# Frequency-domain 7x7 convolution: the last tile's turn, on chip or by DRAM

## The chip, the core and the metric

The kernel runs on one core of a Trainium2 chip. The core has a matrix engine (TensorE, PE in the profile; its weight loads are PEld), three engines for elementwise work (VectorE = DVE, ScalarE = ACT, GpSimd = POOL), a queue engine that mostly issues transfers (SyncE, SP) and 16 DMA engines. The metric is device time in microseconds of one execution; lower is better.

## The reference

```python
# x: (1, 224, 224, 96) bf16, w: (7, 7, 96, 96) bf16
wp = jnp.pad(w, ((0, H - K), (0, W - K), (0, 0), (0, 0)))
Xf = rfft2(x.astype(float32), axes=(1, 2))
Wf = rfft2(wp, axes=(0, 1))
Yf = jnp.einsum('bhwi,hwio->bhwo', Xf, Wf)
y = irfft2(Yf, s=(H, W), axes=(1, 2)).astype(bfloat16)
```

It is a circular 7x7 convolution of a 224x224 image, from 96 channels to 96 channels.

## The kernel before

The 224 rows are cut into `NJ` = 8 blocks of `B` = 28 rows. Each block, with its 6 rows of halo, is taken along the rows into `NS` = 17 frequencies (real and imaginary part: 34 numbers); along the columns the 7 taps are applied directly. The 224 columns are cut into 7 tiles (`NT`; the last is `TL` = 6) of 32 pixels, which are handled as 16 pairs `w`.

A tile goes through these stages:

- Forward transform (`a_jobs`, `f_jobs`): matmuls of the pixels in `xn` with `Fm`; the results are copied to `xf` by ScalarE or VectorE.
- `jit`: VectorE makes sums and differences of these planes in `J`.
- `b_round(t, s)`, one for each of the 17 frequencies s: TensorE multiplies `J` and `xf` with the transformed weights `WF` into two PSUM banks; ScalarE makes `tt_` of the first bank, VectorE makes `u` and `v`, and `ysum` adds them, on GpSimd or, where `ydve` is set, on VectorE. The result has 128 partitions (16 pairs x 8 blocks).
- Turn: the inverse transform contracts over the frequencies, so these have to get from the free dimension to the partitions. In tiles 0 to 5 the result is collected in `yf` (three frequencies a buffer, four buffers), stored to a DRAM tensor `scr`, and loaded from there into `tt` by `load_t`.
- Inverse transform (`c_jobs`): matmuls of `tt` with `G`, copies to `yo`, outputs to DRAM. Eleven such jobs belong to a tile; they run between the rounds of the next tile. `CQ[t]` says how many of the older and of the newer jobs run within the rounds of tile t; `queue_c` starts the loads of a tile.

Each engine takes its instructions in the order in which the program issues them (`_Ordered`). Nearly all transfers are issued by SP, one after the other: a transfer whose wait is not yet over holds those behind it.

The last tile has no next tile to hide its inverse transform. Before the change its turn is made on chip. `b_round` writes the sums of frequencies 0 to 12 (`SA` = 13) into `YA`, which lies in the free `xn`, and those of 13 to 16 into `YB`, in the free `xf` buffer, in an order in which 32x32 blocks can be transposed. `turn_a` (four VectorE transposes of 128x768, the first after the planes of round 13, the last within round 16) makes `TA` of `YA`; `turn_b` (two of 128x384, after the last round) makes `TB` of `YB`. In the tail `first` multiplies `TA` with `GA` (one matmul of 384 columns) and `second` adds four matmuls of 96 columns on `TB` with the four `GB`; there are 16 of each pair (8 blocks, 2 halves), and a copy to `tt` buffers by VectorE and ScalarE in turn follows each `second`. Eight `first` are issued ahead. Outputs are issued by SP, GpSimd and, the last, ScalarE. `GA` and `GB` lie in `GY`, 112 columns each (4 x 28 rows), built by `g_parts` during tiles 3 and 4. `warm` issues two matmuls that only keep TensorE busy.

In the profile every instruction carries the line of the recording helper (L86 before, L89 after), so operations are told apart by their tiles and shapes.

Of the kernel before, what the change touches and what calls it, by code (L numbers as in the profile page):

```python
# [8 lines left out]
BF16 = mybir.dt.bfloat16  # L9
F32 = mybir.dt.float32  # L10
# [4 lines left out]
B = 28  # L15
L = B + KT - 1
LC = L - 2
NS = L // 2
# [15 lines left out]
YGRP = ((0, 3), (3, 6), (6, 9), (9, 12), (12, 15), (15, 17))  # L34
SA = 13
NB4 = 4
YMAX = 3
YBUF = 4
JGB = ((0, 3), (3, 6), (6, 9), (9, 12), (12, 15), (15, 17))
LAG = 4  # L40
CQ = {2: (11, 0), 3: (11, 2), 4: (9, 5), 5: (6, 8), 6: (3, 8)}
SH2 = (0, 8, 13, 17)
MERGE = ()
NP2 = 0
# [9 lines left out]
def kernel(  # L54
# [85 lines left out]
    G = cpool.tile([3 * FR, 3 * B], BF16, name="Gm")  # L140
    SR = 32
    SRB = 2 * (NS - SA)
    assert 2 * SA <= SR and NB4 * SRB == SR and 4 * NJ == SR and B <= SR
    XW = 2 * TW * C
    xn_all = cpool.tile([128, 2 * (XW + 32)], BF16, name="xn")
    xn_bufs = [xn_all[0:R, i * (XW + 32):(i + 1) * (XW + 32)] for i in range(2)]
# [363 lines left out]
    def b_round(t, s, mid, end, ydve=False, planes=()):  # L510
# [5 lines left out]
            1: (Jb[:, 6], Jb[:, 3], Jb[:, 2]),  # L516
            2: (Jb[:, 5], Jb[:, 1], Jb[:, 0]),
        }
        if t == TL:
            yt, i = (YA, 2 * s) if s < SA else (YB, 2 * (s - SA))  # L520
            ym = yt[:, :, i:i + 2, :].rearrange("p g r o -> p g (r o)")
        else:
            for (y0, y1) in YGRP:
                if s == y0:
                    yf_cur[t] = (yf_pool.tile([128, YMAX, 2, 2, C], BF16, name="yf"), y0, y1)
            yf, y0, y1 = yf_cur[t]
            ym = yf[:, s - y0].rearrange("p r m o -> p m r o")
# [13 lines left out]
        if s in REAL:  # L541
            for part in range(2):
                conv(b0, part * C, 0, part)
            if t == TL:
                SE.copy(out=tt_.rearrange("p (r m o) -> p r m o", r=2, m=2),
                        in_=b0[:, 0:2 * C].rearrange("p (r o) -> p r o", o=C).unsqueeze(2).to_broadcast([128, 2, 2, C]))
            else:
                SE.copy(out=tt_[:, 0:2 * C], in_=b0[:, 0:2 * C])
            mid()
            for mi, m in enumerate((2, 1)):  # L550
                for part in range(2):
                    conv(b1, (part * 2 + mi if t == TL else mi * 2 + part) * C, m, part)
            if t == TL:
                VE.tensor_tensor(out=yp(ym), in0=pairs(tt_[:]), in1=pairs(b1[:, 0:4 * C]), op=ALU.add)
            else:
                VE.tensor_tensor(out=ym,
                                 in0=tt_[:, 0:2 * C].rearrange("p (r o) -> p r o", o=C).unsqueeze(1).to_broadcast([128, 2, 2, C]),
                                 in1=b1[:, 0:4 * C].rearrange("p (m r o) -> p m r o", m=2, r=2), op=ALU.add)
# [5 lines left out]
        else:  # L564
            v = tv_pool.tile([128, 2, 2, C], F32, name="v")
            if merge:
                conv(b0, 2 * C, 0, 0, both=True)
                conv(b0, 2 * C, 2, 0, add=True)
                conv(b0, 3 * C, 1, 0, add=True)
                conv(b0, 0, 0, 1)  # L570
                conv(b0, C, 0, 2)
                SE.mul(out=tt_[:], in_=b0[:, 0:4 * C], mul=-0.5)
                u, pr = tt_[:, 2 * C:4 * C].rearrange("p (m o) -> p m o", m=2), tt_[:, 0:2 * C]
            else:
                for part in range(3):
                    conv(b0, part * C, 0, part)
                conv(b0, 3 * C, 2, 0)
                conv(b0, 4 * C, 1, 0)
                u = tv_pool.tile([128, 2, C], F32, name="u")
                if t == TL:  # L580
                    SE.mul(out=tt_[:, 0:C], in_=b0[:, 0:C], mul=-0.5)
                    SE.copy(out=tt_[:, C:3 * C], in_=b0[:, C:3 * C])
                    load["a"] += 240
                else:
                    SE.mul(out=tt_[:, 0:3 * C], in_=b0[:, 0:3 * C], mul=-0.5)
                pr = tt_[:, C:3 * C]
# [3 lines left out]
            mid()  # L590
            for mi, m in enumerate((2, 1)):
                for pi, part in enumerate((1, 2)):
                    conv(b1, (pi * 2 + mi if t == TL else mi * 2 + pi) * C, m, part)
            if t == TL:
                VE.tensor_tensor(out=v[:], in0=pr.rearrange("p (r o) -> p r o", r=2).unsqueeze(2).to_broadcast([128, 2, 2, C]),
                                 in1=b1[:, 0:4 * C].rearrange("p (r m o) -> p r m o", r=2, m=2), op=ALU.add)
            else:
                VE.scalar_tensor_tensor(out=v.rearrange("p m r o -> p m (r o)"),
                                        in0=pr.unsqueeze(1).to_broadcast([128, 2, 2 * C]), scalar=-2.0,
                                        in1=b1[:, 0:4 * C].rearrange("p (m q) -> p m q", m=2), op0=ALU.mult, op1=ALU.add)  # L600
            def ysum(eng):
                if t == TL:
# [13 lines left out]
            load["a"] += 490 if merge else 410  # L616
            load["v"] += (560 if ydve else 250 if t < 2 else 0) + (560 if merge else 900)
            end()
        if t != TL and s == y1 - 1:
            dma(scr_tiles[t].rearrange("w j s e -> (w j) s e")[:, y0:y1], yf[:, 0:y1 - y0].rearrange("p s r m o -> p s (r m o)"))  # L620

    scr_tiles = {}
    tt_tiles = {}
# [14 lines left out]
    NA, NBL = C * SR * 2, C * SRB * 2  # L638
    xs = xf_bufs[(TL + 1) % 2].rearrange("c p r s w j -> c (p r s w j)")
    assert NA + 2 * NBL <= 4 * NS * POS * NJ and NA <= 2 * (XW + 32)  # L640
    YA = xn_all[:, 0:NA].rearrange("p (g s o) -> p g s o", s=SR, o=2)
    TA = xs[:, 0:NA].rearrange("p (g w j e) -> p w j g e", j=NJ, w=4, e=4)
    TB = xs[:, NA:NA + NBL].rearrange("p (g w j e) -> p w j g e", j=NJ, w=4, e=4)
    YB = xs[:, NA + NBL:NA + 2 * NBL].rearrange("p (g s o) -> p g s o", s=SRB, o=2)

    def turn(src, dst, g0, g1):
        load["v"] += 120 + 2 * SR * (g1 - g0) / 0.96
        VE.transpose(out=dst.bitcast(F32).rearrange("p (g n k) -> p g k n", n=SR, k=2)[:, g0:g1], in_=src[:, g0:g1])

    def turn_a(i):  # L650
        src = xn_all[:, 0:NA].bitcast(F32).rearrange("p (g k s) -> p g k s", k=2, s=SR)
        turn(src, xs[:, 0:NA], i * C // 8, (i + 1) * C // 8)

    def turn_b():
        load["v"] += 240 + C // NB4 * SR / 0.96
        src = xs[:, NA + NBL:NA + 2 * NBL].bitcast(F32).rearrange("p (g b k s) -> p k g b s", b=NB4, k=2, s=SRB)
        dst = xs[:, NA:NA + NBL].bitcast(F32).rearrange("p (g b j k) -> p k g b j", b=4, j=NJ, k=2)
        for k in range(2):
            VE.transpose(out=dst[:, k], in_=src[:, k])

    def g_parts():
        for q in range(4):
            dma(GX[q * SR:q * SR + 2 * SA, 0, q * B:q * B + B], G[0:2 * SA, 0:B])
            yield
        for q in range(4):
            for b in range(NB4):
# [1 line left out]
                dma(GX[r:r + SRB, 1 + b, q * B:q * B + B], G[2 * SA:2 * NS, 0:B])  # L668
                yield
        for k in range(NB4 + 1):  # L670
            GE.tensor_copy(out=GY[:, k].rearrange("p (m q) -> p q m", q=4), in_=GX[:, k].rearrange("p (q m) -> p q m", q=4))
            yield

    yo_free = [J_bufs[2][0:4 * B, i * PXC * C:(i + 1) * PXC * C] for i in range(2)]
# [120 lines left out]
    for r in range(NS + LAG):  # L795
# [18 lines left out]
        if r == PGRP[-2][1] + 1:  # L814
# [4 lines left out]
            yo_pool = ctx.enter_context(tc.tile_pool(name="yo", bufs=2, side="right"))  # L819
            g_pool = ctx.enter_context(tc.tile_pool(name="gp", bufs=1, side="right"))  # L820
            GX = g_pool.tile([128, 1 + NB4, 4 * B], BF16, name="GX")
            GY = g_pool.tile([128, 1 + NB4, 4 * B], BF16, name="GY")
            GA, GB = GY[:, 0], GY[:, 1:]
            GE.memset(GX[:], 0.0)
        if r == NS + 3:
            queue_c(0)
        for t in range(2):
# [14 lines left out]
    gp = g_parts()  # L842
    for t in range(2, NT):
        if t == TL:
            GE.memset(YA[:, :, 2 * SA:, :].rearrange("p g s o -> p g (s o)"), 0.0)
        else:
            scr_tiles[t] = dr_pool.tile([TW, NJ, NS, 4 * C], BF16, name="scr")
        qs = []
# [14 lines left out]
        for s in range(NS):  # L863
            now = ()
            if s in plan:
                g = plan[s]
                now = jit(t, g + 1) if g + 1 < len(JGB) else jit(t + 1, 0)
            if s == 3:
                queue_c(t - 1)
            if t in (3, 4):  # L870
                next(gp, None)
            mid = fills(qs, 2 * s)
            if t == TL and s >= SA:
                if s < NS - 1:
                    now = [lambda i=s - SA: turn_a(i)]
                else:
                    mid = lambda m=mid: (m(), turn_a(3))
            b_round(t, s, mid, fills(qs, 2 * s + 1), bool(now) and not (t == TL and s >= SA), now)
    turn_b()
    load["v"] = 2 * BIAS + load["a"]  # L880
    for f in cj:
# [8 lines left out]
    MO = 4 * B  # L890

    def first(j, h):
        pc = bank()[0:MO, 0:NC]
        TE.matmul(pc.rearrange("p (w g e) -> p w g e", w=2, e=4), lhsT=GA, rhs=TA[:, 2 * h:2 * h + 2, j], start=True, stop=False)
        return pc

    def second(j, h, pc, yo):
        po = pc.rearrange("p (w g b e) -> p b w g e", w=2, b=NB4, e=4)
        for b in range(NB4):
            TE.matmul(po[:, b], lhsT=GB[:, b], rhs=TB[:, 2 * h:2 * h + 2, j], start=False, stop=b == NB4 - 1)  # L900
        tail_evac(yo[0:MO, (j % 2) * 2 * NC + h * NC:(j % 2) * 2 * NC + (h + 1) * NC], pc, NC)
    order = [(j, h) for j in range(NJ) for h in range(2)]
    warm(WARM0)
    live = {k: first(*k) for k in order[:8]}
# [44 lines left out]
```

## Time and profile before

| | |
|---|---|
| median of 3 runs | 265.53 us (264.64 to 265.67) |
| the profiled execution's own time | 266.41 us |
| its span, first to last instruction | 264.7 us |
| TensorE matmul, busy | 252.5 us (95%), 5160 instructions |
| VectorE | 215.8 us (82%) |
| ScalarE | 198.6 us (75%) |
| GpSimd | 101.5 us (38%) |
| granted TensorE clock, mean | 0.993 |
| SP's DMA queue (q1) | 41044 packets, 41.98 MB, 56.6% of 16 engines |

The span is shorter than the time by what lies around the program. Busy shares are means over the whole; where time can be lost is seen from which wait ends last in a stretch. A row of a timeline has the start and the length in us, the engine, the operation, out<-in with partitions x elements, the count, and in brackets the idle time before it and what ended it. "128*112" at a matmul means 128 rows and 112 columns of the loaded matrix. Rows of SPq are the issue of a transfer, not the transfer.

### The profile page before, as it was taken

To read this page: it belongs to the slowest core of one execution; us is meant where nothing else is said; L and a number is where in the kernel's file an instruction comes from. 1 tells how busy PE (TensorE), PEld (TensorE's weight loads), DVE (VectorE), ACT (ScalarE), POOL (GpSimd) and SP (SyncE) were. 2 spreads that over 40 slices of the span, in tenths; PEclk is the share of its full clock that TensorE was granted. 3 is DMA by queue.
4 is the path that set the end of the run, shared out by engine and by line. 5 is a ranking of instruction groups with operands and counts; after the bars stand their busy time and mean duration, and the time that the engine had idled before them with its cause. 6 is when DMAs were issued, how large, how long until landed. Compare 5 with 4: busy or idle time off the path is not lost.

```text
span 264.7 us, 12207 instructions
## 1 busy us (share of the span) xinstructions
PE 252.5 (95%) x5160; PEld 234.3 (89%) x5160; DVE 215.8 (82%) x459; ACT 198.6 (75%) x500; POOL 101.5 (38%) x166
## 2 busy tenths in 40 slices
PE   8799998999999999999999999999999999999981
PEld 3569898999999999998999998999999999999861
DVE  5729799898978979977888788777978889899981
ACT  5529997659795566898988869989798886666652
POOL 7781033345355553234123332543143222424420
PEclk9999999999999999999999999999999999999997
DMA  6766210451111299896979449597959753585135
GB/s 162 182 192 152 73 51 2 154 159 47 50 47 47 85 254 208 239 268 180 290 226 244 150 108 315 180 258 185 325 193 206 209 186 125 145 169 155 55 111 175
DMA packets 41416, 43.44 MB, mean 164 GB/s; under 512 B 30836, under 2 KB 33104, under 8 KB 41362
## 3 DMA queue, kind: packets, MB, share of 16 engines
q1 hardware_dynamic: 41044, 41.98, 56.6%
q8 instruction: 40, 0.66, 1.1%
q0 software_dynamic: 192, 0.52, 0.7%
q10 hardware_dynamic: 126, 0.17, 0.2%
q14 instruction: 14, 0.11, 0.1%
HBM read 22.09 MB, written 19.66 MB: 158 GB/s over the span
## 4 chain that ended last, share of the span: by engine, by line
PE 82%; ACT 5%; DVE 4%; issue 3%; DMA 3%; POOL 1%; SPq 1%; DVEq 0%; ACTq 0%
PE pb L86 82%; ACT WF L86 3%; DMA WF<-in_x_dram 3%; DVE WF L86 1%; ACT xf L86 1%; POOL yf L86 1%; DVE J L86 1%; DVE u L86 1%; DVE xf L86 1%; SPq L86 1%; DVE yf L86 0%; ACT tt L86 0%; DVE v L86 0%; ACT tt__676 L86 0%; ACT tt__2951 L86 0%
## 5 line engine op out<-in xcount | busy, mean ns | idle before, releaser
L86 PE MATMUL pb<-WF,J 96*128 96x96 bf16 x2821 | 162.6, 206 | 0.5 <-DVE WF L86 0.3
L86 PEld LDWEIGHTS <-J 96*128 96x128 bf16 x2821 | 137.9, 98 | 8.7 <-DVE u L86 1.5
L86 POOL TENSOR_TENSOR yf<-v,u 128x384 bf16<-128x384 f32 x70 | 69.1, 1001 | 129.5 <-issue 69.2
L86 ACT CAST xf<-pb 96x408 bf16<-96x408 f32 (+3 forms) x143 | 67.2, 487 | 10.3 <-PE pb L86 8.5
L86 PE MATMUL pb<-WF,xf 96*128 96x96 bf16 x952 | 60.2, 206 | 1.1 <-ACT xf L86 0.5
L86 DVE TENSOR_TENSOR J<-xf 96x1824 bf16<-96x1824 bf16 (+1 forms) x84 | 57.5, 724 | 0.1
L86 PEld LDWEIGHTS <-xf 96*128 96x128 bf16 x952 | 47.3, 98 | 1.9 <-issue 0.9
L86 PE MATMUL pb<-Fm,xn 118*128 118x136 bf16 (+3 forms) x640 | 45.5, 199 | 0.9 <-DVE u L86 0.8
L86 ACT CAST WF<-pb 96x480 bf16<-96x480 f32 (+1 forms) x59 | 29.0, 573 | 5.0 <-PE pb L86 5.0
L86 PE MATMUL pb<-tt,Gm 102*84 102x384 bf16 (+1 forms) x132 | 32.1, 326 | 0.0
L86 PEld LDWEIGHTS <-xn 118*128 118x128 bf16 x640 | 30.5, 97 | 1.2 <-issue 1.2
L86 ACT CAST yo<-pb 84x384 bf16<-84x384 f32 (+1 forms) x66 | 28.2, 484 | 2.9 <-PE pb L86 2.6
L86 ACT CAST J<-pb 84x384 bf16<-84x384 f32 (+1 forms) x65 | 28.0, 484 | 2.8 <-PE pb L86 2.8
L86 DVE TENSOR_TENSOR J<-J 96x912 bf16<-96x912 bf16 (+2 forms) x42 | 22.8, 542 | 0.0
L86 PE MATMUL pb<-wq 98*128 98x120 bf16 (+1 forms) x288 | 21.2, 225 | 0.0
L86 PEld LDWEIGHTS <-wq 98*128 98x128 bf16 x288 | 19.4, 148 | 0.2
L86 PE MATMUL pb<-wu 128*128 128x512 bf16 x43 | 11.8, 435 | 1.1 <-DVE ct L86 1.1
L86 DVE TENSOR_TENSOR yf<-v,u 128x384 bf16<-128x384 f32 x20 | 11.3, 567 | 0.7
L86 PEld LDWEIGHTS <-Gm 102*84 102x84 bf16 (+1 forms) x132 | 11.1, 117 | 0.8
L86 DVE CAST WF<-pb 96x480 bf16<-96x480 f32 (+1 forms) x13 | 7.5, 610 | 5.4 <-PE pb L86 5.2
L86 POOL TENSOR_TENSOR xn<-v,u 128x384 bf16<-128x384 f32 x8 | 7.2, 926 | 11.8 <-DVE v L86 11.8
L86 ACT COPY xf<-xf 96x816 bf16<-96x816 bf16 (+3 forms) x20 | 11.2, 621 | 0.0
(404 smaller groups left out, 254.3 us busy)
## 6 DMA issues: line engine op xcount, KB each, us to landing
scr<-yf SPq DMA_DIRECT2D x30, 288.0 KB
xn<-in_x_dram SPq DMA_DIRECT2D x12, 672.0 KB
tt<-scr SPq DMA_DIRECT2D x24, 336.0 KB
out_dram<-yo SPq DMA_DIRECT2D x12, 252.0 KB
out_dram<-J SPq DMA_DIRECT2D x12, 252.0 KB
tt<-scr SPq DMA_DIRECT2D x6, 288.0 KB
WF<-in_x_dram SPq DMA_DIRECT2D x2, 672.0 KB
scr<-yf SPq DMA_DIRECT2D x6, 192.0 KB
```

What stands on the lines that cost most here:

```text
L86: r = fn(*a, **k)
```

## The change

In the last tile frequencies 0 to 12 now go by DRAM as in the other tiles, with a layout of their own; frequencies 13 to 16 are still transposed on chip.

- `b_round`: the special order of sums (`turned`) holds for frequencies 13 to 16 alone; 0 to 12 use the ordinary code and `yf`, in groups `YGT`, and each group is stored to a DRAM tensor of 26 x 128 x 192 when its last frequency is done: 384-byte pieces.
- `rows_a` loads that tensor into `TW4` (in `xn`): each of 26 rows becomes four partitions of 4 pieces of 3 KB. `ROWS` says which frequencies are loaded at which round: 0 to 7 at 12, 8 and 9 at 13, 10 and 11 at 14, 12 at 14.
- The four `turn_a` and the memset of `YA` are gone. The sum of round 15 goes to VectorE.
- `first` contracts over 104 rows (`KA`) instead of 128, with another order of rows in `GX`.
- `GY` has 128 columns a matrix, the last 16 zero; `first` writes 128 partitions of PSUM.
- `CQ[6]` is (3, 9) instead of (3, 8): one job more of tile 5 runs within the rounds, one less behind them. The loads of tile 5 are queued at round 2 instead of 3.

```diff
+YGT = ((0, 3), (3, 6), (6, 8), (8, 10), (10, 13))
+ROWS = ((0, 8, 12), (8, 10, 13), (10, 12, 14), (12, 13, 14))
+GAP = 16
-CQ = {2: (11, 0), 3: (11, 2), 4: (9, 5), 5: (6, 8), 6: (3, 8)}
+CQ = {2: (11, 0), 3: (11, 2), 4: (9, 5), 5: (6, 8), 6: (3, 9)}
...
+    KA = 4 * 2 * SA
...
-        if t == TL:
-            yt, i = (YA, 2 * s) if s < SA else (YB, 2 * (s - SA))
-            ym = yt[:, :, i:i + 2, :].rearrange("p g r o -> p g (r o)")
+        turned = t == TL and s >= SA
+        if turned:
+            i = 2 * (s - SA)
+            ym = YB[:, :, i:i + 2, :].rearrange("p g r o -> p g (r o)")
         else:
-            for (y0, y1) in YGRP:
+            for (y0, y1) in YGT if t == TL else YGRP:
...
-        if t != TL and s == y1 - 1:
-            dma(scr_tiles[t].rearrange("w j s e -> (w j) s e")[:, y0:y1], yf[:, 0:y1 - y0].rearrange("p s r m o -> p s (r m o)"))
+        if not turned and s == y1 - 1:
+            if t == TL:
+                dma(scr_tiles[t].rearrange("a p e -> p a e")[:, 2 * y0:2 * y1], yf[:, 0:y1 - y0].rearrange("p s r m o -> p (s r) (m o)"))
+            else:
...
-    def turn_a(i):
-        src = xn_all[:, 0:NA].bitcast(F32).rearrange("p (g k s) -> p g k s", k=2, s=SR)
-        turn(src, xs[:, 0:NA], i * C // 8, (i + 1) * C // 8)
+    TW4 = xn_all[:, 0:NA].rearrange("p (w f) -> p w f", w=4)[:, :, 0:NJ * 2 * C]
+    TA = TW4.rearrange("p w (j e) -> p w j e", j=NJ)
...
+    def rows_a(s0, s1):
+        av = scr_tiles[TL].rearrange("a (q p) e -> (a q) (p e)", q=4)[8 * s0:8 * s1]
+        dma(TW4[8 * s0:8 * s1], av.rearrange("p (w f) -> p w f", w=4))
...
-            GY = g_pool.tile([128, 1 + NB4, 4 * B], BF16, name="GY")
+            GY = g_pool.tile([128, 1 + NB4, 128], BF16, name="GY")
...
+            GE.memset(GY[:, :, 4 * B:], 0.0)
...
-            GE.memset(YA[:, :, 2 * SA:, :].rearrange("p g s o -> p g (s o)"), 0.0)
+            scr_tiles[t] = dr_pool.tile([2 * SA, 128, 2 * C], BF16, name="scra")
...
-            if s == 3:
+            if s == (2 if t == TL else 3):
                 queue_c(t - 1)
+            for r0, r1, ra in ROWS if t == TL else ():
+                if s == ra:
+                    rows_a(r0, r1)
...
-            mid = fills(qs, 2 * s)
-            if t == TL and s >= SA:
-                if s < NS - 1:
-                    now = [lambda i=s - SA: turn_a(i)]
-                else:
-                    mid = lambda m=mid: (m(), turn_a(3))
-            b_round(t, s, mid, fills(qs, 2 * s + 1), bool(now) and not (t == TL and s >= SA), now)
+            b_round(t, s, fills(qs, 2 * s), fills(qs, 2 * s + 1), bool(now) or t == TL and s == NS - 2, now)
...
-        pc = bank()[0:MO, 0:NC]
-        TE.matmul(pc.rearrange("p (w g e) -> p w g e", w=2, e=4), lhsT=GA, rhs=TA[:, 2 * h:2 * h + 2, j], start=True, stop=False)
+        pc = bank()[:, 0:NC]
+        TE.matmul(pc.rearrange("p (w e) -> p w e", w=2), lhsT=GA[0:KA], rhs=TA[0:KA, 2 * h:2 * h + 2, j], start=True, stop=False)
```

More of the change, by code (lines that the diff above doesn't have):

```diff
@@ L142 @@
     SRB = 2 * (NS - SA)
-    assert 2 * SA <= SR and NB4 * SRB == SR and 4 * NJ == SR and B <= SR
+    assert NB4 * SRB == SR and 4 * NJ == SR and B <= SR and YGT[-1][1] == SA
+    KA = 4 * 2 * SA
     XW = 2 * TW * C
@@ L543, in b_round @@
                 conv(b0, part * C, 0, part)
-            if t == TL:
+            if turned:
                 SE.copy(out=tt_.rearrange("p (r m o) -> p r m o", r=2, m=2),
@@ L551, in b_round @@
                 for part in range(2):
-                    conv(b1, (part * 2 + mi if t == TL else mi * 2 + part) * C, m, part)
-            if t == TL:
+                    conv(b1, (part * 2 + mi if turned else mi * 2 + part) * C, m, part)
+            if turned:
                 VE.tensor_tensor(out=yp(ym), in0=pairs(tt_[:]), in1=pairs(b1[:, 0:4 * C]), op=ALU.add)
@@ L579, in b_round @@
                 u = tv_pool.tile([128, 2, C], F32, name="u")
-                if t == TL:
+                if turned:
                     SE.mul(out=tt_[:, 0:C], in_=b0[:, 0:C], mul=-0.5)
@@ L592, in b_round @@
                 for pi, part in enumerate((1, 2)):
-                    conv(b1, (pi * 2 + mi if t == TL else mi * 2 + pi) * C, m, part)
-            if t == TL:
+                    conv(b1, (pi * 2 + mi if turned else mi * 2 + pi) * C, m, part)
+            if turned:
                 VE.tensor_tensor(out=v[:], in0=pr.rearrange("p (r o) -> p r o", r=2).unsqueeze(2).to_broadcast([128, 2, 2, C]),
@@ L601, in ysum @@
             def ysum(eng):
-                if t == TL:
+                if turned:
                     return eng.tensor_tensor(out=yp(ym), in0=pairs(v.rearrange("p r m o -> p (r m o)")),
@@ L618, in b_round @@
             end()
-        if t != TL and s == y1 - 1:
-            dma(scr_tiles[t].rearrange("w j s e -> (w j) s e")[:, y0:y1], yf[:, 0:y1 - y0].rearrange("p s r m o -> p s (r m o)"))
+        if not turned and s == y1 - 1:
+            if t == TL:
+                dma(scr_tiles[t].rearrange("a p e -> p a e")[:, 2 * y0:2 * y1], yf[:, 0:y1 - y0].rearrange("p s r m o -> p (s r) (m o)"))
+            else:
+                dma(scr_tiles[t].rearrange("w j s e -> (w j) s e")[:, y0:y1], yf[:, 0:y1 - y0].rearrange("p s r m o -> p s (r m o)"))
     scr_tiles = {}
@@ L636, in load_t @@
                 dma(tt[2 * FR:3 * FR, 4 * j:4 * j + 4], sv[r0 + j * FR:r0 + (j + 1) * FR, 12:16])
-    NA, NBL = C * SR * 2, C * SRB * 2
+    NA, NBL = 4 * (NJ * 2 * C + GAP), C * SRB * 2
     xs = xf_bufs[(TL + 1) % 2].rearrange("c p r s w j -> c (p r s w j)")
[L640 to L648, printed above, removed]
-    def turn_a(i):
-        src = xn_all[:, 0:NA].bitcast(F32).rearrange("p (g k s) -> p g k s", k=2, s=SR)
-        turn(src, xs[:, 0:NA], i * C // 8, (i + 1) * C // 8)
+    assert 2 * NBL <= 4 * NS * POS * NJ and NA <= 2 * (XW + 32) and KA <= R
+    TW4 = xn_all[:, 0:NA].rearrange("p (w f) -> p w f", w=4)[:, :, 0:NJ * 2 * C]
+    TA = TW4.rearrange("p w (j e) -> p w j e", j=NJ)
+    TB = xs[:, 0:NBL].rearrange("p (g w j e) -> p w j g e", j=NJ, w=4, e=4)
+    YB = xs[:, NBL:2 * NBL].rearrange("p (g s o) -> p g s o", s=SRB, o=2)
+    def rows_a(s0, s1):
+        av = scr_tiles[TL].rearrange("a (q p) e -> (a q) (p e)", q=4)[8 * s0:8 * s1]
+        dma(TW4[8 * s0:8 * s1], av.rearrange("p (w f) -> p w f", w=4))
     def turn_b():
         load["v"] += 240 + C // NB4 * SR / 0.96
-        src = xs[:, NA + NBL:NA + 2 * NBL].bitcast(F32).rearrange("p (g b k s) -> p k g b s", b=NB4, k=2, s=SRB)
-        dst = xs[:, NA:NA + NBL].bitcast(F32).rearrange("p (g b j k) -> p k g b j", b=4, j=NJ, k=2)
+        src = xs[:, NBL:2 * NBL].bitcast(F32).rearrange("p (g b k s) -> p k g b s", b=NB4, k=2, s=SRB)
+        dst = xs[:, 0:NBL].bitcast(F32).rearrange("p (g b j k) -> p k g b j", b=4, j=NJ, k=2)
         for k in range(2):
@@ L662, in g_parts @@
         for q in range(4):
-            dma(GX[q * SR:q * SR + 2 * SA, 0, q * B:q * B + B], G[0:2 * SA, 0:B])
+            dma(GX[q:KA:4, 0, q * B:q * B + B], G[0:2 * SA, 0:B])
             yield
@@ L670, in g_parts @@
         for k in range(NB4 + 1):
-            GE.tensor_copy(out=GY[:, k].rearrange("p (m q) -> p q m", q=4), in_=GX[:, k].rearrange("p (q m) -> p q m", q=4))
+            GE.tensor_copy(out=GY[:, k, 0:4 * B].rearrange("p (m q) -> p q m", q=4), in_=GX[:, k].rearrange("p (q m) -> p q m", q=4))
             yield
@@ L900, in second @@
             TE.matmul(po[:, b], lhsT=GB[:, b], rhs=TB[:, 2 * h:2 * h + 2, j], start=False, stop=b == NB4 - 1)
-        tail_evac(yo[0:MO, (j % 2) * 2 * NC + h * NC:(j % 2) * 2 * NC + (h + 1) * NC], pc, NC)
+        tail_evac(yo[0:MO, (j % 2) * 2 * NC + h * NC:(j % 2) * 2 * NC + (h + 1) * NC], pc[0:MO], NC)
     order = [(j, h) for j in range(NJ) for h in range(2)]
```

## The prediction

> **What bounds the kernel now.** I read the chain of waits first, in order of time, then the timelines of TensorE, VectorE and SyncE around its last steps.
>
> ```profile
> 159.87 90.96 PE pb L86 x1826
> 250.83 1.82 DVE xf L86 x2
> 252.65 0.14 issue
> 252.78 1.49 PE pb L86 x8
> 254.27 4.36 PE pb L86 x64
> 258.66 0.89 ACT tt L86 x2
> ```
>
> Columns are start, length, what. Up to 250.83 us TensorE alone sets the time. Then the last two transposes of the last tile (DVE) hold the tail back; 8 `first` matmuls follow, then 64 `second` among which the other 8 `first` stand, then the last evacuations. Only the stretch from 250.83 can be shortened by this change, since TensorE's work before it is the same in both kernels. TensorE in that stretch:
>
> ```profile
> 250.16 1.14 PE L86 MATMUL pb<-tt,Gm 102*84 102x384 bf16 x6
> 251.14 0.60 PE L86 MATMUL pb<-wu 128*128 128x512 bf16 x2
> 252.78 6.25 PE L86 MATMUL pb<-xf,GY 128*112 128x384 bf16 x80 [1.05 <-DVE xf L86]
> ```
>
> The last matmul of round 16 stands just before 250.16; six leftover matmuls of the tile before and two warming ones follow; the bracket says that TensorE then idles 1.05 us for VectorE. VectorE:
>
> ```profile
> 245.35 0.56 DVE L86 TENSOR_TENSOR xn<-v,u 128x384 bf16<-128x384 f32 x1
> 250.36 0.54 DVE L86 TENSOR_TENSOR v<-tt__7453,pb 128x384 f32<-128x384 f32 x1
> 250.82 1.82 DVE L86 STREAM_TRANSPOSE xf<-xn 128x768 f32<-128x768 f32 x2
> 252.56 0.51 DVE L86 TENSOR_TENSOR xf<-tt__7497,pb 128x384 bf16<-128x384 f32 x1
> 253.18 1.04 DVE L86 STREAM_TRANSPOSE xf<-xf 128x384 f32<-128x384 f32 x2
> ```
>
> The first row is the sum of frequency 12, the last one that goes by DRAM in the changed kernel: done at 245.91. The 1.82 row is turn_a 2 and 3, which `first` waits for; the 1.04 row is turn_b, done at 254.22, which `second` (254.27) waits for.
>
> **The change part by part.**
>
> *Four turn_a transposes go* (about 0.95 us each: the pair above takes 1.82, two more start at 247.63 and 249.23). VectorE's tail becomes u and v of round 15, its sum (0.56, now on VectorE instead of GpSimd, whose sum is 0.93), the sum of 16 (0.51) and turn_b (1.04). In the trace u of round 15 starts at 250.12 behind a transpose; its matmuls allow about 249.4. From 249.4: 0.3 + 0.54 + 0.56 gives 250.8; round 16's matmuls end some 0.33 later than now (next part), about 250.7, so its sum ends near 251.4 and turn_b near 252.5.
>
> *TensorE's own order.* CQ moves one leftover job (2 of the 6 matmuls, 0.33 us at the pace of that row) into the rounds; the sum until the warming matmuls end is unchanged. Six matmuls starting 0.163 apart end at 251.14, two of 512 columns add 0.43: TensorE is free at 251.57. If the data is there, `first` starts 252.78 - 251.57 = 1.21 us earlier. The 8 `first` take 8 x 0.163 = 1.31 us instead of 1.49 if turn_b is done by then (251.57 + 1.31 = 252.88 against 252.5: it is): 0.18 us more.
>
> *The data now comes by DRAM*: five stores and four loads on SP's queue (the words of the change say three loads; the table has 64, 16, 16 and 8 rows, the last two both waiting for the last store). Only the last store and the loads behind it can be late. The stores of frequencies 0 to 9 are spread over 20 us before; the 64-row load is issued at round 12, about 244. SP's order there is: the 64-row load, an output, the last store, the 16-row load, then the two that wait. The last store follows the sum, at 246.0. Behind the two waiting loads stand only outputs, which nobody waits for in the tail. What the trace shows of such a transfer:
>
> ```profile
> 225.36 0.35 SPq L86 DMA_DIRECT2D scr<-yf  x1
> 228.55 0.33 SPq L86 DMA_DIRECT2D tt<-scr  x1
> 251.40 0.32 SPq L86 DMA_DIRECT2D out_dram<-J  x1
> ...
> DMA packets 2230, 0.84 MB, mean 222 GB/s; under 512 B 2230, under 2 KB 2230, under 8 KB 2230
> q1 hardware_dynamic: 2230, 0.84, 106.4%
> DMA packets 135, 0.18 MB, mean 168 GB/s; under 512 B 15, under 2 KB 135, under 8 KB 135
> q1 hardware_dynamic: 135, 0.18, 45.8%
> ```
>
> The first pair of DMA rows is the stretch 229.4 to 233.2, loads of 384 B packets: 106.4% of 16 x 3.8 us over 2230 packets is 29 ns each. The second is 225.9 to 227.0, a store of 1536 B packets: 60 ns each. The new stores write 384 B packets, 768 of them, 48 an engine: a write that short is not in the trace; 29 and 60 ns bound it, 1.4 to 2.9 us. Both known transfers begin to move 0.8 us after their issue; I add 0.3 us until the semaphore is seen. So the store has landed at 248.5 to 250.0, with 45 ns, midway, at 249.25. The second waiting load is issued 0.35 us behind the first. The output issued at 251.40 had moved its 84 packets of 3 KB by 253.4, 2.0 us; a load of 64 and one of 32 packets should take some 1.8. That gives 250.65 to 252.15, by the middle 251.4: just under TensorE's 251.57. But one row says more: the store of 225.36 held its reader until 228.55, 3.2 us where 0.8 + 8 packets of 60 ns + 0.3 makes 1.6. An instruction fetch stood on one of the engines then (q8 in the same view: one packet, 15.5% of 16 x 0.6 us, 1.5 us long). Another such fetch stands at 250.4 for about 0.95 us, beside the new loads; where it hits them, that is rival A.
>
> [...]
>
> *Matrices of 128 columns.* The 96-column matmuls with the 112-column GY start 51 ns apart (15 of them in 0.93 us, the last 0.21 long); those on J, with 128 columns and the same 96 moving, 43 (21 in 1.06 us). The load rows fit:
>
> ```profile
> L86 PEld LDWEIGHTS <-GY 128*112 128x112 bf16 x80 | 5.4, 131 | 2.3 <-POOL xf L86 1.5 <-issue 0.2
> L86 DVE CAST tt<-pb 112x384 bf16<-112x384 f32 x8 | 4.2, 553 | 1.1 <-PE pb L86 1.0
> L86 PEld LDWEIGHTS <-wu 128*128 128x128 bf16 x2 | 0.2, 98 | 0.1
> ```
>
> 64 x 8.5 ns = 0.54 us of TensorE. It can't all be had: VectorE's eight evacuations of 0.553 back to back take 4.42 us from 0.36 after the first `second`, 4.8 in all, where the last evacuation now ends 259.55 - 254.27 = 5.28 after. So 0.44. The lower bound is 0: the new 112-to-128 step may not be what paces them (`second` writes 4-element pieces). And the eight outputs behind them already get in each other's way: the three on GpSimd take 3.7 us to land (median). I give half of it back: 0.22.
>
> *At no cost:* the memset of GY's last 16 columns per matrix (GpSimd, in the first two tiles, where GpSimd is idle half the time; 0.2 us if not); fewer ScalarE pieces in frequencies 1 to 12 (0.41 instead of 0.46, under TensorE); the memset of xn that goes (1.05 us, under TensorE); the added stores' traffic before 244, beside loads that are needed 2 us and more later. Without that cover they cost a wait of TensorE for the tile before's rows, at most the 0.3 us a store holds SP, each.
>
> *Sum:* 1.21 + 0.18 + 0.22 = 1.6 us off the profiled span of 264.7, so 263.1. That execution took 266.41, 0.9 above the runs' median of 265.53; I take the 1.6 off the median: **263.9**. With all at its best it is 1.21 + 0.18 + 0.44 = 1.8 (263.7); with the loads at the late end, 252.15, it is 0.63 + 0.18 + 0.22 = 1.0 (264.5).
>
> **Rivals.**
>
> *A. The wait changes its name.* The loads land at 252.4 to 253.3 (a fetch on one of the store's or the loads' engines), so TensorE idles for DMA what it idled for VectorE. For: the 3.2 us row. Against: no fetch lies between 245.0 and 250.3 in this trace, when the store moves. With `first` at 252.8 it is 0 + 0.18 + 0.22: 265.1.
>
> *B. Slower: the short stores write far slower than short loads read.* Price: each 10 ns of a packet is 0.48 us of the last store. From 60 ns the start moves from 252.15; the kernel is slower than before when `first` starts after 252.78 + 0.40, that is from about 82 ns a packet; at 115 ns it starts at 254.8, 2.0 late less 0.40, and the time is 267.1. For: nothing in the trace writes under 512 B in this volume, and the last 64-row load and the store share the rings. Against: the 1536 B stores, at 60 ns, move 26 GB/s an engine, so writing as such is not slow. [...]
>
> *C. The new columns bring nothing* (`second` stays at 51 ns), the rest as forecast: 1.21 + 0.18 gives 264.1. For: nothing in the trace writes such pieces from 128 columns. Against: the 98 ns load.
>
> **Chances.** Forecast 0.50 (263.9, own range 263.4 to 264.5), A 0.22, B 0.18, C 0.10. A difference below about 0.5% (1.3 us) can't be told from none here, so faster means under 264.2: three quarters of the forecast case and half of C, 0.43; slower (over 266.9) is most of B and what I have not thought of, 0.17; the same 0.40. Range 263.3 to 266.4: it leaves out the far half of B and little at the fast end.
>
> **What would show it.** Right: no transposes 128x768 in the last tile; TensorE's gap before the GY matmuls under 0.3 us; the 64 `second` 43 ns apart with VectorE casting without a pause; the last store's issue near 246.0 and the two last loads' near 249.3. Wrong: a gap of 1 us or more whose releaser is a DMA (A), with loads issued after 251 (B), or `second` at 51 ns (C). It would all be wrong if TensorE showed gaps before 250, waiting for the tile before's rows behind the new stores.

## The result

| | changed | before |
|---|---|---|
| median | 272.66 us (272.06 to 273.14, 4 runs) | 265.41 us (264.64 to 265.67, 4 runs) |
| the profiled execution's own time | 272.44 us | 266.41 us |
| its span | 270.7 us | 264.7 us |
| granted TensorE clock, mean | 0.979 | 0.993 |

The changed kernel is 2.8% slower: ratio 1.0278, 95% interval 1.0261 to 1.0296. The forecast was 263.9 us.

### The profile page after: what moved, and what is told of

It reads as the page before. It is cut to its first block, busy times and chain, and to the rows that moved or that the text cites. A ratio compares the mean times of both kernels' runs of the same rounds, so it can differ in the third digit from the quotient of the medians.

```text
span 270.7 us, 12209 instructions
## 1 busy us (share of the span) xinstructions
PE 255.0 (94%) x5160; PEld 234.8 (87%) x5160; DVE 213.0 (79%) x456; ACT 197.9 (73%) x488; POOL 99.7 (37%) x165
## 4 chain that ended last, share of the span: by engine, by line
PE 78%; DVE 6%; ACT 5%; DMA 4%; issue 3%; POOL 1%; SPq 0%; POOLq 0%; DVEq 0%; ACTq 0%
PE pb L89 78%; ACT WF L89 3%; DMA scra<-yf 2%; DVE WF L89 2%; DMA xn<-scra 2%; DVE J L89 2%; ACT xf L89 1%; DVE u L89 1%; POOL yf L89 1%; DVE v L89 1%; DVE yf L89 0%; SPq L89 0%; POOLq L946 0%; DVE tt L89 0%; ACT tt__676 L89 0%
## 5 line engine op out<-in xcount | busy, mean ns | idle before, releaser
L89 POOL TENSOR_TENSOR yf<-v,u 128x384 bf16<-128x384 f32 x78 | 76.9, 1000 | 143.5 <-issue 72.5
L89 PEld LDWEIGHTS <-GY 128*128 128x128 bf16 (+1 forms) x80 | 5.7, 116 | 9.9 <-issue 9.3
L89 DVE TENSOR_TENSOR yf<-v,u 128x384 bf16<-128x384 f32 x24 | 13.6, 565 | 0.8
L89 PE MATMUL pb<-wu 128*128 128x512 bf16 x43 | 12.7, 459 | 1.1 <-DVE ct L89 1.1
L89 DVE CAST tt<-pb 112x384 bf16<-112x384 f32 x8 | 4.4, 556 | 10.4 <-PE pb L89 9.9
L89 PE MATMUL pb<-xn,GY 104*128 104x384 bf16 x16 | 5.6, 442 | 7.3 <-DMA xn<-scra 7.3
L89 ACT CAST tt<-pb 112x384 bf16<-112x384 f32 x8 | 3.7, 480 | 11.4 <-PE pb L89 11.3
```

What stands on the lines that cost most here:

```text
L89: r = fn(*a, **k)
```

## The profile after

The chain of waits of the changed kernel, from the last store on (columns: start, length, what):

```profile
246.00 6.59 DMA scra<-yf
252.59 0.02 issue
252.61 0.57 SPq L89
...
253.23 4.57 DMA xn<-scra
257.80 0.14 issue
257.93 6.75 PE pb L89 x58
264.68 0.02 issue
264.70 0.57 DVE tt L89
```

Before the change this place read 1.82 us of VectorE, 1.49 of `first`, 4.36 of `second`. Now two transfers in a row stand there, the last store (6.59 us from issue to landing) and the last load behind it (4.57). What VectorE and SP did ahead of that store (the first row is the sum of frequency 12, the second the issue of the 64-row load):

```profile
244.60 0.56 DVE L89 TENSOR_TENSOR yf<-v,u 128x384 bf16<-128x384 f32 x1
244.75 0.53 SPq L89 DMA_DIRECT2D xn<-scra  x1
245.39 0.52 SPq L89 DMA_DIRECT2D out_dram<-J  x1
246.00 0.39 SPq L89 DMA_DIRECT2D scra<-yf  x1
```

The sum was done at 245.16. The store was issued 0.84 us later, because SP held an output of `J` ahead of it until ScalarE had written its data (245.80). TensorE's timeline shows what the wait for the two transfers costs:

```profile
250.00 0.60 PE L89 MATMUL pb<-wu 128*128 128x512 bf16 x2
257.93 2.72 PE L89 MATMUL pb<-xn,GY 104*128 104x384 bf16 x8 [7.34 <-DMA xn<-scra]
260.44 1.81 PE L89 MATMUL pb<-xf,GY 128*128 128x96 bf16 x20
```

The bracket is an idle time of 7.34 us, where it was 1.05. The eight `first` then take 2.5 us (257.93 to 260.44) instead of 1.49. Why shows in the busy times by stretch (columns: busy time and count of PE, PEld, DVE, ACT, POOL, then the granted TensorE clock, the share of the 16 DMA engines, GB/s):

```profile
251.00:252.00 1.00, 0.00 (x0) 0.00 (x0) 0.64 (x2) 0.32 (x1) 0.00 (x0) 1.00 1.08 308
252.00:253.00 1.00, 0.00 (x0) 0.00 (x0) 0.00 (x0) 0.00 (x0) 0.00 (x0) 0.85 0.27 35
253.00:254.00 1.00, 0.00 (x0) 0.00 (x0) 0.00 (x0) 0.00 (x0) 0.00 (x0) 0.50 0.10 18
262.00:263.00 1.00, 1.00 (x11) 0.70 (x9) 0.77 (x2) 0.52 (x2) 0.08 (x1) 0.53 0.00 0
263.00:264.00 1.00, 1.00 (x17) 0.80 (x16) 0.56 (x1) 0.72 (x2) 0.80 (x1) 1.00 0.51 126
```

The clock fell to half while TensorE idled and came back only about 5 us after the first `first`. In the kernel before it stayed at 1.00 over the idle time ahead of `first`:

```profile
252.00:253.00 1.00, 0.22 (x2) 0.21 (x3) 1.00 (x2) 0.90 (x3) 0.00 (x0) 1.00 0.69 197
```

One difference is not the change. TensorE was free at 250.60 here and at 251.74 before. This row of the waits of the kernel before has no counterpart after:

```profile
PE pb L86 <- DMA WF<-in_x_dram: 1.6, 1, 1.6
```

It is a wait at the start of the program, for the weights, of that one execution; it shifts its whole tail. So the profiles differ by 6.0 us and the medians by 7.25.

The span's 6.0 us add up: `first` starts 5.15 us later (257.93 against 252.78), and from there to the end it is 12.8 us instead of 11.9, 0.85 more.

## The experiments

All ratios are to the kernel before, with 95% intervals. "Store" is the flight (issue to landing) of the last store, "load" that of the last load that waits for it.

| run | median, us | ratio | store | load | `first` at |
|---|---|---|---|---|---|
| changed kernel | 272.66 | 1.0278 (1.0261 to 1.0296) | 6.59 | 4.57 | 257.93 |
| e1: before, 128 columns | 265.42 | 1.0004 (0.9991 to 1.0018) | | | 251.45 |
| e2: 64 rows behind the store | 272.56 | 1.0272 (1.0242 to 1.0303) | 2.71 | 8.44 | 257.02 |
| e3: 36 warming matmuls | 271.46 | 1.0231 (1.0208 to 1.0253) | 6.38 | 4.56 | 257.68 |
| e4: no 64-row load | 268.29 | 1.0104 (1.0083 to 1.0125) | 2.60 | 4.37 | 253.70 |
| e5: spread, first try | 275.62 | 1.0393 (1.0354 to 1.0432) | 4.99 | 2.83 | 261.83 |
| e6: the same, store first | 273.65 | 1.0305 (1.028 to 1.033) | 2.56 | 5.08 | 259.19 |
| e12: spread, same order | 270.71 | 1.0214 (1.018 to 1.0248) | 4.36 | 3.21 | 256.09 |
| e9: spread, store first | 269.46 | 1.0152 (1.0111 to 1.0192) | 2.73 | 4.85 | 254.86 |
| e10: spread, 48 rows early | 269.56 | 1.0172 (1.014 to 1.0203) | 3.33 | 4.29 | 255.01 |
| e11: 48 rows early, blocks | 271.65 | 1.0236 (1.0202 to 1.027) | 5.12 | 4.70 | 256.73 |
| e13: e10 and warming | 268.32 | 1.0126 (1.0091 to 1.0161) | 4.36 | 4.26 | 255.43 |
| e14: last 24 rows only | 267.83 | 1.0097 (1.0071 to 1.0124) | 2.54 | 4.28 | 252.93 |
| e15: as e14, older rows | 267.93 (one run) | | 2.94 | 4.71 | 253.05 |
| e8a: half outputs, 112 | 263.85 | 0.9942 (0.9928 to 0.9955) | | | 251.35 |
| e8b: half outputs, 128 | 263.77 | 0.9934 (0.9919 to 0.9948) | | | 252.34 |

### What stands ahead of the last store: e2 and e4

```diff
 e2
-ROWS = ((0, 8, 12), (8, 10, 13), (10, 12, 14), (12, 13, 14))
+ROWS = ((0, 8, 13), (8, 10, 13), (10, 12, 14), (12, 13, 14))
 e4
+ROWS = ((8, 10, 13), (10, 12, 14), (12, 13, 14))
```

> The changed kernel with the 64-row load issued one round later, just behind the last store instead of ahead of it; the same packets in all. Theory (ring order: the last store stands behind the 64-row load on SP's queue): the last store lands at 248.3 to 249 instead of 252.59, the two waiting loads are issued before 250, but now stand behind the 64-row load and land at 253 to 255; first at about 254 instead of 257.9, time about 268 to 269.5. Rival 1 (384 B writes are slow in themselves, or DMA is short of rate whatever the order): the store lands after 250.5 and the time stays at 271 to 273. Rival 2 (loads that wait are slow by their own packets): the store lands at 248.5 but each load still takes over 4 us with nothing ahead of it.

> The changed kernel without its 64-row load (frequencies 0 to 7 of the last tile are left out of the output). Theory (the 64-row load ahead of the last store in the rings is the whole delay): the last store lands at 248.2 to 249, the waiting loads are issued 248.5 to 249.3 and land near 251, TensorE idles under 0.5 us ahead of the firsts, time 263.8 to 265.5, the prediction's own. Rival (short writes or the waiting loads are slow by themselves): the store lands after 250 or the loads take over 4 us, time over 267.

Chain of waits of e2:

```profile
245.10 2.71 DMA scra<-yf
...
248.45 8.44 DMA xn<-scra
...
257.02 5.89 PE pb L89 x58
```

Chain of waits of e4:

```profile
245.95 2.60 DMA scra<-yf
...
249.19 4.37 DMA xn<-scra
...
253.70 5.99 PE pb L89 x58
```

With the 64-row load behind it, or without that load, the last store lands in 2.6 to 2.7 us instead of 6.59. In e2 nothing was changed but the load's place in SP's queue, so the store's 4 us more in the changed kernel are those of standing behind that load. The price I had feared for short writes is not there either: in the 0.8 us from 247.0 of e14, where only the store moves, 547 packets of 384 B took 100.1% of 16 engines, 23 ns each.

But e2 gained nothing where I expected 268 to 269.5, and e4 stopped at 268.3 where I expected the forecast's own time. The loads behind the store are slow too: 4.37 us with nothing large ahead, and 8.44 with the 64 rows ahead. The expectation's second rival for e2 was right in part.

### Why the loads are slow: rows in a block, or spread

The 64-row load goes to partitions 0 to 63, the waiting ones to 80 to 95 and 96 to 103. Here is how the 64-row load moves in the changed kernel (transfers between 246.5 and 249.5 us):

```profile
DMA packets 203, 0.62 MB, mean 208 GB/s; under 512 B 0, under 2 KB 0, under 8 KB 203
q1 hardware_dynamic: 203, 0.62, 98.7%
```

The engines were full (98.7%), yet moved 208 GB/s; a packet of 3 KB took 233 ns (98.7% of 16 x 3.0 us over 203), where the fastest in the trace take 121. That the block of neighbouring partitions holds the rate is a guess of mine here, which nothing in this trace shows. The experiment lays the same rows 2 or 4 partitions apart:

```diff
+RUNS = ((0, 64, 0, 2), (64, 80, 3, 4), (80, 104, 1, 4))
-        dma(TW4[8 * s0:8 * s1], av.rearrange("p (w f) -> p w f", w=4))
+        av = av.rearrange("p (w f) -> p w f", w=4)
+        for r0, r1, p0, st in RUNS:
+            lo, hi = max(r0, 8 * s0), min(r1, 8 * s1)
+            if lo < hi:
+                p = p0 + st * (lo - r0)
+                dma(TW4[p:p + st * (hi - lo - 1) + 1:st], av[lo - 8 * s0:hi - 8 * s0])
```

`GX` is filled in the same order, and `first` contracts over 128 rows. A first form (e5, e6) laid the rows in five groups, with partitions 4 apart:

> The changed kernel with the 104 rows of the waiting matrix laid out 4 partitions apart (row r of a run on partition 4r + run number, the tail matrix permuted alike), so that every load reaches partitions 0 to 103 instead of one block of neighbours; same rows, same issue order, same packets of 3 KB. [...] Rival 1 (the packets are slow on the side of DRAM, just written or 12 KB apart): flights and time stay, 271.5 to 273.5. Rival 2 (the store's 384 B writes and the order alone set the wait): same as rival 1 for the loads behind the store.

> The spread rows, and besides the 64-row load issued just behind the last store and the last 24 rows in one load. [...]

Both times were spoiled by the edit itself: it added fourteen small copies into `GX` to SP's queue in tiles 3 and 4, TensorE idled there (8.77 of 10 us busy from 190 to 200, where it was 10.00), and the last store of e5 was issued at 253.27. Their flights could still be read: in e5 the last load took 2.83 us instead of 4.57, and in e6, with the store first, the last store landed 2.56 us behind its issue. The second form needs eight more copies than the changed kernel and one transfer from DRAM:

> The spread rows without the two dozen small copies that held up the tiles before in the first try: the 64-row load on the even partitions 0 to 126, the next 16 rows on 3, 7, 11 and so on, the last 24 on 1, 5, 9 and so on; order of issues as in the changed kernel. [...] Rival (DRAM side): 271.5 to 273.5.

The transfers of e12 between 248 and 249.75 us, where only its 64-row load moves:

```profile
DMA packets 197, 0.61 MB, mean 346 GB/s; under 512 B 0, under 2 KB 0, under 8 KB 197
q1 hardware_dynamic: 197, 0.61, 93.4%
```

The same packets from the same DRAM rows, 133 ns each instead of 233 and 346 GB/s instead of 208; only the partitions they go to were changed. The two waiting loads landed 2.88 and 3.21 us behind their issue instead of 3.96 and 4.57. So the partitions alone made this difference; by what, no run shows. The time fell by 1.95 us, although in the profiled execution the last store was issued 1.8 us later than in the changed kernel (247.81). Most of that is not the edit's doing: at the start of this execution TensorE waited 0.6 us for `WF` and 0.6 us for `wq`, which it did not in the profiled execution of the changed kernel, while the copies into `GX` begin only at 131.9.

### Order and partitions together: e9, e10, e11, e13

```diff
 e9
+ROWS = ((0, 8, 13), (8, 10, 13), (10, 13, 14))
 e10 (spread) and, as (0, 6, 11), (6, 10, 13), (10, 13, 14), e11 (blocks as in the changed kernel)
+ROWS = ((0, 6, 11), (6, 8, 13), (8, 10, 13), (10, 13, 14))
 e13: e10, the copies into GX for GA issued by GpSimd, and
-WARM0 = 2
+WARM0 = 12
```

> The same spread, with the 64-row load issued behind the last store and the last 24 rows in one load. [...] Rival (bytes in the tail, 1.3 MB at some 200 GB/s whatever the partitions): first at 255 or later, time over 268.

> The same spread, with 48 rows (frequencies 0 to 5) loaded one round earlier than the 64 were, and the rows of frequencies 6 to 9 behind the last store, the last 24 in one load. Theory: the 48 rows move at 244 to 246.3, before the store, so that behind the store stand 32 and 24 rows only; the 24 rows land at 250.5 to 251.5, TensorE idles under 1 us, time 263.5 to 265.5. Rival (the backlog of stores and loads that fills the engines until 244 grows by these rows and the store waits for it): the store lands after 249.5, first after 253, time over 267.

> The same order as the kernel before in this list, but rows in blocks of neighbouring partitions as in the changed kernel (48, 32 and 24 rows). [...] Rival (order is all): the same time as with spread rows.

> All remedies together: spread rows, 48 rows one round earlier, 32 rows behind the last store, the last 24 in one load, the tail matrix's small copies on GpSimd's queue instead of SP's, and 12 warming matmuls. [...] Rival (two transfers in a row through DRAM cost over 7 us at the end whatever their order): first after 254, time over 267.5.

e10 missed: 269.6 instead of 263.5 to 265.5. e9, at 269.5, came out near its rival (`first` at 254.86). The store did land in 2.7 and 3.3 us, but the last 24 rows took 4.85 and 4.29. e11 is 2.1 us slower than its spread twin e10, so order is not all, against its rival. e13 has all remedies, and is still 1.3% slower than before; its rival was right. Its chain (of an execution of 269.75 us, slower than its median):

```profile
246.65 4.36 DMA scra<-yf
251.01 0.02 issue
251.03 4.26 DMA xn<-scra
...
255.43 5.96 PE pb L90 x58
```

The store's 4.36 us here look like rival A of the prediction: 15 of its 16 landings (the trace has 16 for a transfer) were in by 249.97, and the last came at 251.01, while an instruction fetch that began at 250.04 took 1.16 us. The trace does not say which engine the fetch was on. The 12 warming matmuls ended at 252.71; TensorE then idled 2.71 us, and the granted clock was 0.50 from 256.37 to 259.78 all the same.

### The floor of the way through DRAM: e14 and e15

e14 is e13 with 2 warming matmuls and one load, `ROWS = ((10, 13, 14),)`. e15 lets this load read rows 0 to 23 of the same DRAM tensor instead of 80 to 103, still behind the last store:

```diff
-...rearrange("a (q p) e -> (a q) (p e)", q=4)[8 * s0:8 * s1]
+...rearrange("a (q p) e -> (a q) (p e)", q=4)[0:24]
+                tc.add_manual_dep(d.ins, stored[0].ins.name, SYNC, reason="behind the last store")
```

> The same spread and queues, 2 warming matmuls, with only the last 24 rows loaded (frequencies 0 to 9 of the last tile are left out of the output). It measures the floor of the way through DRAM: last store 2.6 us, load with nothing ahead of it in the rings. Theory (the prediction's flight of 1.8 us was too short even for an idle queue): the load lands 2.4 to 3.2 us behind its issue, first at 251.3 to 252.2, time 264 to 265.5. Rival (a flight of 1.8 is to be had when nothing is ahead): first at 250.6 to 251.

> As the kernel with the last 24 rows only, but the load that waits for the last store reads rows of frequencies 0 to 2, written 12 us before, instead of the rows just written (these rows are then missing in the output). Theory (the flight of 4.3 us is that of a load of this form into an idle queue, whatever it reads): 4.0 to 4.6 us again. Rival (rows read right behind their writing come slowly): 2 to 3 us, TensorE idle under 1 us.

Chain of e14:

```profile
245.91 2.54 DMA scra<-yf
...
248.51 4.28 DMA xn<-scra
...
252.93 5.97 PE pb L90 x58
```

With nothing ahead of either, a store and a load that depends on it take 2.54 + 4.28 us. My expectation of 2.4 to 3.2 us for the load was still too short. So `first` starts at 252.93 even with 80 of the 104 rows left out. In e8a, which has the on-chip turn and whose TensorE waited as long at the start as that of e14 (1.1 us for `WF` in both), it starts at 251.35. With a store and a load that fly as these two do, no order of the other transfers brings `first` to that point.

It is not quite the floor, though. In e9, e10, e13 and e14 the last 24 rows come in one load; in e5 and e12 they come in two, as in the changed kernel. From the store's landing to that of the last row it is 3.5 us in e5 and 3.8 in e12, but 4.3 to 4.9 with one load. So joining the loads did not help, and no run sets the two forms side by side with all else equal. From a store issued right behind its sum (245.20, e15), 2.54 us of store (e14) and 3.5 us of loads (e5), I estimate `first` at 251.3: level with e8a, not ahead of it.

That the rows had just been written is not the reason for the long load: older rows took 4.71 us in e15, one run, a little over the 4.0 to 4.6 expected. The transfers of e14 from 250 to 251.25 us, the load's first stretch:

```profile
DMA packets 53, 0.18 MB, mean 141 GB/s; under 512 B 0, under 2 KB 0, under 8 KB 52
q1 hardware_dynamic: 52, 0.16, 66.8%
q8 instruction: 1, 0.02, 4.8%
```

The first packet moves 1.6 us behind the start of the issue (0.85 of it is SP's issuing itself, where the store took 0.39), then one of the load's packets takes 257 ns on average (66.8% of 16 x 1.25 us over 52) before the pace gets to 121, and an instruction fetch of 0.96 us holds one engine. Which of these is at fault for the rest stays open.

### The clock: e3

```diff
-WARM0 = 2
+WARM0 = 36
```

> The changed kernel with 36 warming matmuls of 512 columns instead of 2 ahead of the tail, so that TensorE works while it waits for the loads. Theory (part of the loss is the clock that falls to half while TensorE idles 7.3 us): the firsts start at the same 257.9, 0.163 apart instead of 0.31, the clock row stays at 0.9 or more, and the time falls by 1 to 2.5 us, to 270 to 271.6; the rest of the loss is the wait itself. Rival (the tail is bound by evacuations and outputs, the clock costs nothing): no change, 272.7.

TensorE's timeline of e3:

```profile
249.91 7.93 PE L89 MATMUL pb<-wu 128*128 128x512 bf16 x36
257.68 1.47 PE L89 MATMUL pb<-xn,GY 104*128 104x384 bf16 x8
258.98 1.02 PE L89 MATMUL pb<-xf,GY 128*128 128x96 bf16 x20
```

At full clock the first eight take 1.3 us again and the last evacuation by VectorE ends 6.2 us after the first `first` (263.89) instead of 8.5 (266.40). Of these 2.3 us 1.2 reach the median (272.66 to 271.46): the last output landed 4.7 us behind its issue instead of 3.3, since the eight outputs now come closer together (SP issues its four from 260.0 to 263.5, in the changed kernel from 261.8 to 266.1).

### The columns and the outputs: e1, e8a, e8b

e1 is the kernel before with `GY` of 128 columns and nothing else. e8a and e8b are the kernel before and e1 with half of each output at the end:

```diff
-out[0, j * B:(j + 1) * B, w0:w0 + 2 * TW, :] ... in_=yo[0:MO,
+out[0, j * B:j * B + B // 2, w0:w0 + 2 * TW, :] ... in_=yo[0:MO // 2,
```

> The kernel before with nothing changed but the tail matrices of 128 columns (112 used, 16 zero). Theory (term of the prediction): the 64 second matmuls start 43 ns apart instead of 51, 0.54 us of TensorE, of which 0.2 to 0.45 us reaches the end; ratio to before 0.998 to 0.9995, the last evacuation ends 4.8 to 5.1 us after the first second instead of 5.28. Rival (C of the prediction): the pitch stays 51 ns and the time too.

> The kernel before (112 columns) with only 14 of the 28 rows of each of the last tile's eight outputs written (the other half is left out). Theory (at the end the eight outputs of 172 KB queue on the DMA engines, each landing some 1.3 us behind the one before, and hold the end): the last output lands 2.5 us behind its issue instead of 4.1, time 263.2 to 264.4. Rival (the evacuations set the end, outputs only follow at a fixed distance): 265.4 as before.

> The same half outputs with tail matrices of 128 columns. Theory (the columns make the evacuations end 1 us and more sooner, and with full outputs the queue of outputs ate it): 0.6 to 1.5 us below the half-output kernel with 112 columns, 262.2 to 263.4. Rival (the columns bring nothing anywhere): the same time as the half-output kernel with 112 columns, within 0.3 us.

Timelines of e1, TensorE and VectorE:

```profile
251.45 5.81 PE L86 MATMUL pb<-xf,GY 128*128 128x384 bf16 x80 [1.08 <-DVE xf L86]
253.31 4.50 DVE L86 CAST tt<-pb 112x384 bf16<-112x384 f32 x8 [0.42 <-PE pb L86]
```

The matmuls take 5.81 us instead of 6.25, and VectorE's eight evacuations stand back to back, as forecast. The last evacuation ends 6.37 us after the first `first` instead of 6.77, 0.40 us sooner. But from the first `first` to the landing of the last output it is 10.87 us against 10.89: the last output takes 4.44 us from issue to landing instead of 4.09. With half outputs (2.47 us for the last one in both) it is 8.91 (e8b) against 9.27 (e8a), and there 0.36 us arrive. The medians of e8a and e8b differ by 0.08 us only, less than the runs can tell, so the profiles carry this, not the times: the 0.6 to 1.5 us that I expected of e8b did not come. That the outputs hold the end is seen in the times: half of them left out saves 0.6% (e8a).

## Why the prediction was wrong

- **"Only the last store and the loads behind it can be late"**: right as to the place. The gap's releaser is a DMA, and all of TensorE's 7.34 us lie there. That the store was issued at 246.00, as forecast, is luck: the sum was done at 245.16 instead of the 245.91 of the forecast (this execution had no such wait for `WF`), and SP then held the store 0.84 us behind an output that was not ready, a wait that the forecast put at nothing.
- **"So the store has landed at 248.5 to 250.0"**: wrong, 252.59. The sum counted the store's own 48 packets an engine and began 0.8 us after its issue. It left out the 64-row load that SP had issued 1.25 us ahead, 16 packets of 3 KB on each engine, which moved from 246.2 to 250.6. I had named SP's order, but used it only for issue times, not for what the engines still have to move ahead of the store. The store alone takes 2.54 to 2.73 us (e2, e4, e6, e9, e14; 2.94 in e15), a little better than my middle of 3.25. The 0.3 us that the sum adds until the semaphore is seen was an estimate of mine that no run shows: from the last packet of data to the landing it was 0.41 us for GpSimd's last output in the trace of before (262.14 to 262.55), and 0.89 for this store (251.70 to 252.59).
- **"A load of 64 and one of 32 packets should take some 1.8"**: wrong, the two waiting loads took 3.96 and 4.57 us. The model was an output of 84 packets, which goes from 84 partitions to DRAM; these loads go to 16 and 8 neighbouring partitions. Spread rows cut 1.1 and 1.4 us (e12). What is left there, 3.8 us from the store's landing to that of the last row where the sum had 2.15, is the flight of small loads that wait for nothing but the store. Part of it is their start: the sum let a transfer move 0.8 us after its issue, the store did so after 0.9 (e14), but the first packets of the loads came 1.4 us (changed kernel, e12) and 1.6 us (e14) after the first issue. The trace of before shows no such load alone; an upper bound for it was missing from the sum, and the range was too narrow by that. The two terms explain the miss: 3.34 us for the store, and 5.21 instead of 2.15 us from its landing to that of the last load, together 6.4; `first` came 6.36 us after the 251.57 of the sum.
- **"8 x 0.163 = 1.31 us" for the first eight**: 2.5, because the clock fell (0.50 granted from 252.69 to 262.93). An idle TensorE was priced as a wait alone; the clock behind it cost 1.2 us of the median (e3).
- **Matrices of 128 columns, 0.22 us**: the size at the evacuations was right (0.40 measured, 0.44 worked out), the guess that half is given back was too kind: practically all of it is (e1).
- **At no cost, "the added stores' traffic before 244"**: held. TensorE is busy throughout from 160 to 250 us in both profiles, although the engines' share from 236 to 244 rose from 0.69 to 1.05. It is not free, though: with the engines full (1.05), a load asked for earlier did not land earlier by as much. In e11, 48 of the rows asked for at 242.58 landed only at 249.82, and the store still took 5.12 us.
- **Rivals.** A had the right kind, a wait that changes its name, but `first` at 252.8. Its fetch is there, at 252.24 in the changed kernel, but behind the store's packets (the last at 251.7) and before those of the waiting loads (from 253.97), so it does not explain the miss; in e13 it seems to have hit the store. B was slower, but by a mechanism that is not there: a 384 B write took 23 ns (e14), below the lower of the forecast's two bounds (29 and 60). C's outcome, columns that bring nothing, came true in e1, but not its mechanism: the matmuls got faster (5.81 us instead of 6.25), and the outputs ate it.

## What to carry to other kernels

Here a transfer's flight started behind what its issuer had put in the queue before it (the last store landed after 6.59 us behind the 64-row load, after 2.71 ahead of it): to time a store or load near the end, list what was issued in the 5 us ahead of it, with bytes and rate. For a load, look at which partitions it goes to before taking a duration from another transfer; here 64 neighbouring partitions took 208 GB/s, and the same rows on every second partition 346. A turn through DRAM in a tail is two transfers in a row, here 6.8 us with nothing ahead of either (some 6 us by the best parts of different runs, an estimate), and TensorE's clock fell to 0.50 while it waited (7.34 us in the changed kernel, 2.08 in e14); an on-chip transpose of 1.8 us is hard to beat.

## What the runs showed of the hardware

- The clock fell sooner than I would have thought. In e14 TensorE idled only 2.08 us (250.85 to 252.93), and the eight `first` still took 2.5 us. In the trace of the changed kernel the clock changed only at times that lie a multiple of 3.41 us apart (half clock from 252.69 to 262.93, 10.24 us, and again from 269.76); in e14 it was at half for 3.41 us. Stretches cut at these times, of e14, e15 and e3:

```profile
249.52:252.93 3.41, 1.33 (x13) 0.67 (x11) 2.23 (x5) 1.82 (x5) 0.00 (x0) 1.00 0.64 192
252.93:256.34 3.41, 3.41 (x20) 2.06 (x21) 0.34 (x1) 0.01 (x1) 0.00 (x0) 0.50 0.15 50
249.33:252.74 3.41, 1.55 (x17) 0.85 (x14) 2.45 (x5) 2.04 (x5) 0.00 (x0) 1.00 0.66 186
261.66:265.07 3.41, 1.69 (x31) 1.34 (x28) 2.00 (x4) 1.81 (x4) 1.48 (x3) 1.00 0.78 220
```

  TensorE was busy 1.33 us of the stretch in e14 and 1.55 in e15, and the clock fell at its end; in e3 it was busy 1.69, and the clock stayed at 1.00 through the next 3.41 us. In the changed kernel it was at 0.50 through a stretch with 1.59 us of work (256.10 to 259.52) and came back to 1.00 behind one with 3.41 (259.52 to 262.93). So in these stretches 2.08 us (e14) and 1.86 us (e15) without work went with a fall, and 1.72 us (e3) did not. What decides it, and whether a wait of 2 us costs the clock at any place, no run here shows.
- DMA issues that seemed free were not: fourteen more copies of some hundred bytes in SP's queue, 50 us and more ahead of the end, went with TensorE idling from 190 to 200 us (8.77 us busy of 10) and a last store 7 us later (e5). What eight copies and one transfer more cost in e12 can't be told from its waits at the start. With the copies for `GA` on GpSimd's queue the store was issued at 245.91 and 246.65 (e14, e13), 246.00 in the changed kernel, each time behind outputs in SP's queue.
